# Projections of two attention layers: the order of the first segment's k held, the second x of B rounded later, A's shifts in one store, transposes of v a tile later

## The chip, the core and the metric

The kernel runs on one NeuronCore of a Trainium2 chip. The core has a matrix engine (TensorE, PE in the profile, with its weight loads as PEld), a vector engine (VectorE, DVE), an activation engine (ScalarE, ACT), a general engine (GpSimd, POOL) and a sync engine (SyncE, SP) that computes nothing and issues most of the transfers. Each engine has its own queue of instructions, which it runs in order; engines wait for each other through semaphores. SBUF is the on-chip memory of 128 partitions, PSUM the smaller one into which PE writes its sums, and DMA engines move data between SBUF and the DRAM. The metric is the device time of one execution in microseconds; lower is better.

## The reference: what is computed

Two attention layers, A and B, over 2048 positions of width 576, with 32 heads of 18; everything is float32, and the outputs are put side by side.

```python
# A: one k and one v for all heads (multi-query), no mask
q = (x @ wq).reshape(B, S, H, Dh).transpose(0, 2, 1, 3);  k = x @ wk;  v = x @ wv
p = softmax(einsum("bhqd,bkd->bhqk", q, k) * Dh ** -0.5)
a = einsum("bhqk,bkd->bhqd", p, v).transpose(0, 2, 1, 3).reshape(B, S, H * Dh) @ wo

# B: four segments of 512 positions with a memory carried from one to the next
for s in range(4):
    qs, ks, vs = q[:, :, s], k[:, :, s], v[:, :, s]
    logits = einsum("bhqd,bhkd->bhqk", qs, ks) * scale + mask
    a_dot = einsum("bhqk,bhkd->bhqd", softmax(logits), vs)
    a_mem = einsum("bhld,bhde->bhle", phi(qs), M) / (einsum("bhld,bhd->bhl", phi(qs), z)[..., None] + 1e-6)
    outs.append(g * a_mem + (1 - g) * a_dot)
    M = M + einsum("bhld,bhle->bhde", phi(ks), vs);  z = z + einsum("bhld->bhd", phi(ks))
b = stack(outs)... @ wo          # phi(t) = t + 1 if t > 0 else exp(t)
return concatenate([a, b], axis=-1)
```

## The kernel before, in words

The program has two stages. The first, until about 315 us, makes the projections q, k and v of both layers and B's memory, and puts them into DRAM; the second is attention with the output projections. The change touches the first.

**Parts.** To keep float32's accuracy at the faster matmul type, each operand is split into a rounded high part and the rest: x into `xh` and `xl` (`load_xk`, L191 to L203), the weights into `wAh`, `wAl`, `wBh`, `wBl`. A projection tile (`proj`, L232) is 14 matmuls of 512 columns into one PSUM tile `pj` (four buffers): three products for each of four slabs of 128 rows of x and two for the fifth, of 64 rows. Up to 126 rows (seven heads) come out of one tile, so a chunk of 512 positions takes five tiles.

**Layer A** (L250 on) goes through four chunks c, its tiles in the order 4, 0, 1, 2, 3. Tile 4 carries k and v besides four heads of q. ACT copies v's 18 rows to `vT` (L298), PE transposes them (L301, four small matmuls), and DVE copies them to `VA` (L302). Each tile's result is split into `qp` (ACT's cast L111, then DVE's subtraction L112; three buffers) and stored by SP (L116). Meanwhile the next chunk's x is loaded and split; in the last chunk that is B's first.

**A's shifts.** Behind the last chunk PE begins the first projection tile of B's k (`ahead`, L333). An upper bound on the scores follows: the largest k by head is spread over the rows by a matmul (L338), copied to `kAp` (L339), multiplied with a mask into `kbdA` (five steps, L342), and 20 matmuls (L347) make `pu`. From that DVE makes `fm`, `sht` and the two parts `shp` (L350, L121 to L124), which four DMAs issued by ACT store to `shA` (L353).

**Layer B** (L383 on) goes through four segments s. In each come five tiles of k (tile 4 holds the last four heads of q and three of k), eight groups of v (`values`, L457: 14 matmuls each, then ACT's copies to `vch` and `kn` and a store by ACT), and four tiles of q. For a k tile DVE takes the maximum `kmB` (L423), ACT and DVE make `qp` and SP stores it, DVE makes `kbB` (L427), then `phi` (L363): two activations `ph_e` on ACT (L366, L367) and `kf` on DVE (L369). `natural` (L393) transposes kf on PE into the one buffer `tr` (L396), and DVE copies that to `pkN` (L397). At the end of a segment, 20 matmuls (L530) give B's shifts, and `pkN` and `vch` give the memory's increment (L555, L564 on). In segment 0 the weights for q are also still being made ready: a load `wr` issued by POOL (L224), ACT's cast (L229) and POOL's subtraction (L230), one slab for each k tile.

**What sets the order.** In this stage the order of instructions on each engine is not the one written: a scheduler places each by its own estimate of when its operands are ready. `pin` (L177, `tc.keep_in_program_order`) holds those instructions that it is given in the order in which they are written; before the change these are POOL's loads, the casts and subtractions of B's weights, and a few small steps. The second stage is scheduled by hand. At its beginning all engines pass a branch on a flag (L580) that comes from the bounds.

The x of segment 1 has three load buffers `xr`. Its five slabs are written in the loop over the q tiles of segment 0 (`nx[2](t)`, L507); the scheduler puts the rounding of all five among DVE's steps of A's last tile, of A's shifts and of the first k tile.

## Time and profile before

| | us |
|---|---|
| median of 3 runs | 1448.65 |
| the runs | 1448.05 to 1451.8 |
| profiled execution | 1452.01 |
| its span | 1450.0 |
| first stage, to attention's first score matmul | 314.6 |
| PE busy in the span | 1424.0 |
| ACT busy | 1194.9 |
| DVE busy | 1023.9 |

How to read the lines of the profile shown below. A line of the stretches (two times in us with a colon) has the length, then for PE, PEld, DVE, ACT and POOL the busy time in us and the number of instructions, then the granted share of PE's clock, the busy share of the DMA engines and their GB/s. A line of the waits says which engine and line waited for whom: us in total, how often, the longest. A line of the timeline has start and duration in us, engine, line, operation, what it writes and reads, shape, how many were merged, and in brackets the idle time of that engine before it and what ended that. A matmul's duration is that of its way through the array; matmuls overlap, and the distance of their starts is what one costs. Engine names with q are that engine's issuing of transfers.

### The profile page before, as it was taken

To read this page: it belongs to the slowest core of one execution; us is meant where nothing else is said; L and a number is where in the kernel's file an instruction comes from. 1 tells how busy PE (TensorE), PEld (TensorE's weight loads), DVE (VectorE), ACT (ScalarE), POOL (GpSimd) and SP (SyncE) were. 2 spreads that over 40 slices of the span, in tenths; PEclk is the share of its full clock that TensorE was granted. 3 is DMA by queue.
4 is the path that set the end of the run, shared out by engine and by line. 5 is a ranking of instruction groups with operands and counts; after the bars stand their busy time and mean duration, and the time that the engine had idled before them with its cause. 6 is when DMAs were issued, how large, how long until landed. Compare 5 with 4: busy or idle time off the path is not lost.

```text
span 1450.0 us, 40761 instructions
## 1 busy us (share of the span) xinstructions
PE 1424.0 (98%) x17540; PEld 840.9 (58%) x17540; DVE 1023.9 (71%) x1211; ACT 1194.9 (82%) x1429; POOL 245.7 (17%) x324
## 2 busy tenths in 40 slices
PE   9989999999999999999999999999999999999998
PEld 6768878855454555555555555555555555555565
DVE  6663473556776678887777788777778877887761
ACT  4542334259999999999999999999999999999960
POOL 2421000002123312311110160131013300100001
PEclk9999999999999999999999999999999999999999
DMA  9864444457465335332312452123104121110022
GB/s 278 270 215 137 130 162 159 162 165 202 147 175 159 92 97 175 116 108 87 108 57 68 128 154 80 62 100 93 57 26 143 60 74 46 57 42 17 17 87 74
DMA packets 86079, 166.33 MB, mean 115 GB/s; under 512 B 11872, under 2 KB 19673, under 8 KB 85718
## 3 DMA queue, kind: packets, MB, share of 16 engines
q1 hardware_dynamic: 79014, 152.87, 33.8%
q0 software_dynamic: 1664, 4.78, 1.3%
q10 hardware_dynamic: 5216, 6.03, 1.3%
q8 instruction: 138, 2.26, 0.7%
q14 instruction: 47, 0.39, 0.1%
HBM read 96.15 MB, written 67.49 MB: 113 GB/s over the span
## 4 chain that ended last, share of the span: by engine, by line
PE 64%; ACT 8%; DMA 3%; issue 2%; DVE 0%; POOL 0%; SPq 0%; DVEq 0%; POOLq 0%; ACTq 0%
PE O L893 30%; PE E L845 19%; PE F L742 11%; ACT P L863 8%; PE E L854 3%; PE E L742 1%; DMA sm<-oB 1%; PE O L742 1%; DMA rB<-sm 0%; DMA rA<-sm 0%; DMA stA<-qA 0%; DMA stB<-kB 0%; DMA stB<-qB 0%; DMA out<-osb 0%; DMA rb<-rB 0%
## 5 line engine op out<-in xcount | busy, mean ns | idle before, releaser
L863 ACT ACTIVATE P<-E 128x1024 f32<-128x1024 f32 (+1 forms) x800 | 788.4, 1078 | 15.0 <-PE E L845 11.8
L860 DVE COPY W<-E 128x1024 f32<-128x1024 f32 (+1 forms) x384 | 461.0, 1201 | 188.6 <-PE E L845 121.4
L893 PE MATMUL O<-P,VA 128*32 128x256 f32 x7936 | 509.7, 380 | 0.0
L863 ACT ACTIVATE P<-W 128x1024 f32<-128x1024 f32 (+1 forms) x384 | 434.6, 1132 | 1.5 <-DVE W L860 1.5
L893 PEld LDWEIGHTS O<-P,VA 128*32 128x32 f32 x7936 | 262.6, 110 | 146.6 <-issue 9.5
L845 PE MATMUL E<-stA,kstA 56*128 56x512 f32 x1920 | 330.8, 440 | 2.0 <-ACT P L863 1.3
L845 PEld LDWEIGHTS E<-stA,kstA 56*128 56x128 f32 x1920 | 154.6, 184 | 180.8 <-ACT P L863 121.0
L868 POOL TENSOR_SCALAR_AFFINE_SELECT P<-P 128x256 f32<-128x256 f32 (+1 forms) x192 | 94.2, 493 | 447.5 <-ACT P L863 414.7
L729 POOL TENSOR_TENSOR o<-o,rb 126x512 f32<-126x512 f32 (+1 forms) x40 | 60.5, 1518 | 436.8 <-PE F L742 143.5
L742 PE MATMUL F<-woB,o 126*32 126x192 f32 (+1 forms) x1920 | 127.6, 338 | 0.0
L825 DVE SCALAR_TENSOR_TENSOR q<-q,PD 128x1024 f32<-128x1024 f32 x96 | 118.5, 1234 | 0.0
L893 PE MATMUL O<-P,vseg 128*32 128x256 f32 (+2 forms) x1536 | 83.4, 348 | 1.9 <-POOL P L868 1.8
L742 PEld LDWEIGHTS F<-woB,o 126*32 126x32 f32 (+1 forms) x1920 | 38.2, 108 | 70.8 <-issue 61.4
L742 PE MATMUL F<-woA,o 126*32 126x192 f32 (+1 forms) x1240 | 77.7, 338 | 1.3 <-DVE osb L767 1.3
L111 ACT CAST qp<-pj 126x512 fp32r<-126x512 f32 (+1 forms) x54 | 31.3, 583 | 54.6 <-DVE kmB L423 33.2
L239 PE MATMUL pj<-xh,wBh 128*126 128x512 f32 x180 | 75.0, 416 | 0.0
L902 DVE COPY oe<-O 128x512 f32<-128x512 f32 x64 | 44.2, 691 | 41.7 <-PE O L893 39.3
L239 PE MATMUL pj<-xh,wBl 128*126 128x512 f32 x180 | 72.9, 405 | 0.0
L112 DVE TENSOR_TENSOR qp<-pj,qp 126x512 fp32r<-126x512 f32 (+1 forms) x54 | 36.7, 684 | 49.7 <-ACT qp L111 49.6
L854 PE MATMUL E<-stB 56*128 56x256 f32 (+3 forms) x512 | 62.5, 350 | 2.5 <-ACT P L863 2.0
L893 PEld LDWEIGHTS O<-P,vseg 128*32 128x32 f32 x1536 | 48.6, 110 | 27.9 <-issue 3.3
L239 PE MATMUL pj<-xl,wBh 128*126 128x512 f32 x144 | 60.0, 417 | 0.0
(177 smaller groups left out, 1372.7 us busy)
## 6 DMA issues: line engine op xcount, KB each, us to landing
stB<-kB SPq DMA_DIRECT2D x96, 144.0 KB
stB<-qB SPq DMA_DIRECT2D x32, 288.0 KB
stA<-qA SPq DMA_DIRECT2D x30, 288.0 KB
oA<-oe SPq DMA_DIRECT2D x32, 256.0 KB
oB<-oe SPq DMA_DIRECT2D x32, 256.0 KB
qA<-qp SPq DMA_DIRECT2D x16, 504.0 KB
kB<-qp SPq DMA_DIRECT2D x16, 504.0 KB
qB<-qp SPq DMA_DIRECT2D x16, 504.0 KB
```

The costliest lines, as they stand in the source:

```text
L112: nc.vector.tensor_tensor(qp[:R, 1, :n], src, qp[:R, 0, :n].bitcast(F32), op=ALU.subtract)
L239: nc.tensor.matmul(dst, w[:, c0 : c0 + M], x, start=i == 0, stop=i == len(ops) - 1)
L729: steps = [lambda: v.tensor_tensor(o, o, rb, op=ALU.mult)]
L742: nc.tensor.matmul(dst[32 * j : 32 * j + 32], parts[ab, c][: RT[t], t, r0 : r0 + 32], wo[ab][: RT[t], t, c0 : c0 + n], start=start, stop=stop,
L825: steps.append(lambda a=a: v.scalar_tensor_tensor(q, q, a, p, op0=ALU.add, op1=ALU.mult))
L845: nc.tensor.matmul(e[:, j], kstA[rows, 128 * kt : 128 * kt + 128], st[rows, h, :], start=True, stop=True)
L854: nc.tensor.matmul(e[:, j, c0 : c0 + 512 - 128 * k], st[rows, 4 + h, ks], st[rows, h, 128 * k :], start=True, stop=True)
L860: nc.vector.tensor_copy(src[:, :, :n], e[:, :, :n])
L863: nc.scalar.activation(p[:, :, :n], src[:, :, :n], AF.Exp, scale=SCALE)
L868: nc.gpsimd.affine_select(diag, diag, pattern=[[0, 2], [0, m], [1, 128]], base=0, channel_multiplier=-1, compare_op=ALU.is_ge, fill=0.0)
L893: nc.tensor.matmul(o[32 * j : 32 * j + 32, q0 : q0 + n], v, p[:, j % 2, p0 : p0 + n], start=m == hf == 0, stop=last and hf == 1,)
L902: nc.vector.tensor_copy(osb, o)
```

## The change

Four edits in the first stage; the arithmetic is the same.

1. The transposes of v (L301, L302) are written under the next tile, t == 0, not directly behind tile 4. In the built order PE does them 3 to 10 matmuls later in chunks 1 to 3 and at the same place in chunk 0.
2. `shA` becomes one DRAM tensor with all four chunks' rows, and the four stores of ACT one store by SP. In the built order it stands on SP behind the last store of A's q and before the first of B's k.
3. In segment 0 of B, `hold` is `pin`: kmB, both steps of qp, kbB, and phi's three steps stand on their engines in the written order, which now has phi before `split_wpart`. In the built order DVE runs kmB, qp, kbB, kf, pkN of one tile and then those of the next; ACT runs qp, both ph_e and the cast of wr, with the copies of values between. For the later segments nothing of the sequence changes.
4. The split of segment 1's x is written behind the store of each q tile of segment 0, and its rounding is pinned (`behind=True`). In the built order all of it stands on DVE behind that tile's qp, and two of the loads on SP behind stores of q.

POOL's order is the same. PE's order differs from the first stage's chunk 1 to the values of segment 1; transposes of kn (L483) come in the first q tile of segment 0, where they stood among the values. Attention has the same instructions in the same order.

```diff
--- before.py
+++ after.py
@@ -81,7 +81,8 @@
     qB = [dram(f"qB{c}", [H, DH, 2, C], F32) for c in range(NSEG)]
     kB = [dram(f"kB{c}", [H, DH, 2, C], F32) for c in range(NSEG)]
     vB = [dram(f"vB{c}", [L, H * VW], F32) for c in range(NSEG)]
-    shA = [dram(f"shA{c}", [2, H, C], F32) for c in range(NCH)]
+    shAs = dram("shA", [2, NCH * H, C], F32)
+    shA = [shAs[:, H * c : H * c + H] for c in range(NCH)]
     shB = [dram(f"shB{c}", [2, 128, C], F32) for c in range(NSEG)]
     shX = [dram(f"shX{c}", [2, H, C], F32) for c in range(NSEG)]
     oA = [dram(f"oA{c}", [H, 32, C], F32) for c in range(NCH)]
@@ -104,12 +105,12 @@
     fm = cp.tile([128, 5], F32, name="fm")
     nc.gpsimd.memset(fm, 0.0)
 
-    def split2(pool, src, R):
+    def split2(pool, src, R, hold=lambda ins: ins):
 
         n = src.shape[-1]
         qp = pool.tile([128, 2, C], F32R, name="qp", bufs=3)
-        nc.scalar.copy(qp[:R, 0, :n], src)
-        nc.vector.tensor_tensor(qp[:R, 1, :n], src, qp[:R, 0, :n].bitcast(F32), op=ALU.subtract)
+        hold(nc.scalar.copy(qp[:R, 0, :n], src))
+        hold(nc.vector.tensor_tensor(qp[:R, 1, :n], src, qp[:R, 0, :n].bitcast(F32), op=ALU.subtract))
         return qp
 
     def store_parts(qp, r0, R, dst, h0, nh):
@@ -188,13 +189,15 @@
             tile_, c0 = XRAW[c]
             return tile_[:, k, c0 : c0 + C]
 
-        def load_xk(xh, xl, xT, c, k):
+        def load_xk(xh, xl, xT, c, k, behind=False):
             if xT is a_xT and c < 3:
                 xr = xraw(c, k)
             else:
                 xr = px.tile([128, C], F32, name="xr", bufs=3)
                 load_part(xr, xT, c * C, C, k, nc.sync)
-            (nc.scalar.copy if xT is a_xT and c == 0 else nc.vector.tensor_copy)(xh[:, k], xr)
+            rounded = (nc.scalar.copy if xT is a_xT and c == 0 else nc.vector.tensor_copy)(xh[:, k], xr)
+            if behind:
+                pin(rounded)
 
             engine = nc.gpsimd if xT is a_xT and (c, k) == (1, 3) else nc.vector
             if k < 4:
@@ -206,7 +209,7 @@
 
             xh = px.tile([128, 5, C], F32R, name="xh")
             xl = px.tile([128, 4, C], F32R, name="xl")
-            return xh, xl, lambda k: load_xk(xh, xl, xT, c, k)
+            return xh, xl, lambda k, **kw: load_xk(xh, xl, xT, c, k, **kw)
 
         def split_w(wh, wl, wr, c0, n, k, engine):
             nc.scalar.copy(wh[:, k, c0 : c0 + n], wr)
@@ -296,6 +299,8 @@
                     nc.vector.tensor_reduce(km[:M, c : c + 1], pj[:M], axis=AX.X, op=ALU.max, apply_absolute_value=True)
                     vT = p1.tile([128, C], F32, name="vT", bufs=2)
                     nc.scalar.copy(vT[96:114], pj[96:114])
+                if t == 0:
+
                     pv = ps.tile([128, 4, 128], F32, name="tr", bufs=1)
                     for i in range(4):
                         nc.tensor.transpose(pv[:, i, 0:DH], vT[96:114, 128 * i : 128 * i + 128], ident[96:114, 96:114])
@@ -349,8 +354,7 @@
                 )
         nc.vector.tensor_reduce(fm[:, 0:1], pu, axis=AX.X, op=ALU.max)
         sp = shift_parts(pt, pu, -BOUND_UP, C, 128)
-        for c in range(NCH):
-            nc.scalar.dma_start(shA[c].rearrange("j h t -> h j t"), sp[32 * c : 32 * c + 32].bitcast(F32))
+        nc.sync.dma_start(shAs.rearrange("j r t -> r j t"), sp.bitcast(F32))
         wAp.close()
 
 
@@ -360,13 +364,13 @@
         zst = p2.tile([128, 5, 32], F32, name="zst")
         zc = p2.tile([128, 5], F32, name="zc")
 
-        def phi(src, R, nm, bufs):
+        def phi(src, R, nm, bufs, hold=lambda ins: ins):
 
             e = p2.tile([128, C], F32, name="ph_e", bufs=2)
-            nc.scalar.activation(e[:R], src, AF.Relu, scale=-1.0)
-            nc.scalar.activation(e[:R], e[:R], AF.Exp, scale=-1.0)
+            hold(nc.scalar.activation(e[:R], src, AF.Relu, scale=-1.0))
+            hold(nc.scalar.activation(e[:R], e[:R], AF.Exp, scale=-1.0))
             f = p2.tile([128, C], F32, name=nm, bufs=bufs)
-            nc.vector.scalar_tensor_tensor(f[:R], src, 0.0, e[:R], op0=ALU.max, op1=ALU.add)
+            hold(nc.vector.scalar_tensor_tensor(f[:R], src, 0.0, e[:R], op0=ALU.max, op1=ALU.add))
             return f
 
         def loose_flag():
@@ -420,25 +424,27 @@
                     proj(pj[:126], wBh, wBl, xh, xl, 630 + 126 * t if t < 4 else 504, 126)
                 if t and not last:
                     natural(f, pkN[:, t - 1, :, 0:126], 0, 126)
-                nc.vector.tensor_reduce(kmB[:126, t : t + 1], pj[:126], axis=AX.X, op=ALU.max, apply_absolute_value=True)
-                qp = split2(pt, pj[:126], 126)
+
+                hold = pin if s == 0 else lambda ins: ins
+                hold(nc.vector.tensor_reduce(kmB[:126, t : t + 1], pj[:126], axis=AX.X, op=ALU.max, apply_absolute_value=True))
+                qp = split2(pt, pj[:126], 126, hold)
                 if t < 4:
                     store_parts(qp, 0, 126, kB[s], 7 * t, 7)
-                    nc.vector.tensor_scalar(kbB[:126, t], zmask[:126, t], kmB[:126, t : t + 1], None, op0=ALU.mult)
+                    hold(nc.vector.tensor_scalar(kbB[:126, t], zmask[:126, t], kmB[:126, t : t + 1], None, op0=ALU.mult))
                 else:
                     store_parts(qp, 0, 72, qB[s], 28, 4)
                     store_parts(qp, 72, 54, kB[s], 28, 3)
                     magnitude(4, pj)
+                if s and not last:
+                    nx[2](t)
+                if not last or t == 4:
+                    f = phi(pj[:126], 126, "kf" if t < 4 else "qf", 2 if t < 4 else 5, hold)
+                    if t == 4:
+                        fs[4] = f
                 if s == 0:
                     split_wpart(10 + t)
                     if t < 4:
                         load_wpart(11 + t)
-                elif not last:
-                    nx[2](t)
-                if not last or t == 4:
-                    f = phi(pj[:126], 126, "kf" if t < 4 else "qf", 2 if t < 4 else 5)
-                    if t == 4:
-                        fs[4] = f
             if s:
                 from_memory(4)
             if s == 0:
@@ -503,13 +509,13 @@
             for t in range(4):
                 pj = ps.tile([128, C], F32, name="pj", bufs=4)
                 proj(pj[:126], wBh, wBl, xh, xl, 126 * t, 126)
-                if s == 0:
-                    nx[2](t)
-                    if t == 3:
-                        nx[2](4)
                 magnitude(t, pj)
                 qp = split2(pt, pj[:126], 126)
                 store_parts(qp, 0, 126, qB[s], 7 * t, 7)
+                if s == 0:
+                    nx[2](t, behind=True)
+                    if t == 3:
+                        nx[2](4, behind=True)
                 if s:
                     fs[t] = phi(pj[:126], 126, "qf", 5)
                     from_memory(t)
```

## The prediction

> **What bounds the kernel now.** I read the page's first part and its chain first, then the stage before attention in stretches of 20 us, then TensorE's (PE's) own waits there.

> ```profile
> span 1450.0 us, 40761 instructions
> PE 1424.0 (98%) x17540; PEld 840.9 (58%) x17540; DVE 1023.9 (71%) x1211; ACT 1194.9 (82%) x1429; POOL 245.7 (17%) x324
> PE 64%; ACT 8%; DMA 3%; issue 2%; DVE 0%; POOL 0%; SPq 0%; DVEq 0%; POOLq 0%; ACTq 0%
> ...
> 60.00:80.00 20.00, 18.62 (x83) 14.40 (x81) 12.77 (x20) 8.92 (x16) 10.00 (x9) 1.00 0.83 284
> 80.00:100.00 20.00, 14.49 (x69) 10.91 (x70) 15.14 (x34) 5.50 (x11) 3.90 (x5) 0.88 0.67 199
> 100.00:120.00 20.00, 19.32 (x129) 17.59 (x129) 7.65 (x14) 9.72 (x24) 9.62 (x13) 0.95 0.50 143
> ...
> PE nd L347 <- DVE kbdA L342: 3.3, 1, 3.3
> PE tr L396 <- issue: 2.4, 1, 2.4
> PE tr L301 <- ACT vT L298: 1.2, 1, 1.2
> PE E L845 <- SPq L580: 1.1, 1, 1.1
> ```

> PE is busy 98% of the span and carries 64% of the chain, so time is won only where PE waits or runs slowly. Before attention (about 315 us) that is nearly one place: from 60 to 120 us, most of all 80 to 100, where PE is busy 14.49 of 20 us at a granted clock of 0.88. The waits are 3.3 us for kbdA, 2.4 us in front of a transpose of kf, 1.2 us for vT. The clock is a cost of its own:

> ```profile
> 61.20:64.60 3.40, 2.21 (x13) 1.52 (x12) 2.10 (x6) 1.80 (x4) 0.42 (x1) 1.00 0.98 361
> 77.90:81.30 3.40, 1.91 (x10) 1.25 (x8) 1.88 (x4) 0.00 (x0) 0.71 (x1) 1.00 0.65 248
> 81.30:84.70 3.40, 1.59 (x22) 0.87 (x23) 3.16 (x11) 0.00 (x0) 0.20 (x1) 1.00 0.82 267
> 84.80:88.20 3.40, 3.40 (x10) 2.60 (x9) 3.40 (x8) 1.10 (x2) 0.32 (x2) 0.50 0.63 196
> 94.90:98.30 3.40, 1.00 (x8) 0.92 (x8) 2.44 (x5) 2.35 (x5) 1.76 (x2) 1.00 0.30 101
> 98.40:101.80 3.40, 3.40 (x12) 2.75 (x11) 2.58 (x5) 1.64 (x4) 0.11 (x1) 0.51 0.72 230
> ```

> Two stretches of 3.4 us run at half clock, each right behind one in which PE idled 1.8 us (81.3) or 2.4 us (94.9); idling 1.2 and 1.5 us (61.2, 77.9) had no such sequel. A half-clock stretch loses 1.7 us of work. Waits and clock together: 3.3 + 2.4 + 1.2 + 2 x 1.7 = 10.3 us, and that is about all there is to win.

> **Where the two large waits come from.** VectorE (DVE) and ScalarE (ACT) run in order; the built order of the changed kernel shows what stands before what.

> ```profile
> 79.42 0.43 DVE L197 CAST xh<-xr 128x512 fp32r<-128x512 f32 x1 [3.53 <-DMA xr<-b_xT]
> ...
> 82.63 0.15 DVE L339 COPY kAp<-mm 126x1 f32<-126x1 f32 x1
> 82.81 0.82 DVE L342 TENSOR_SCALAR kbdA<-hmask,kAp 126x32 bf16<-126x32 f32 x5
> ...
> 78.50 0.28 PE L338 MATMUL mm<-kmx,sel 114*126 114x1 f32 x2
> 78.64 0.48 PE L239 MATMUL pj<-xh,wBh 128*126 128x512 f32 x1
> 83.11 1.26 PE L347 MATMUL nd<-AQ,kbdA 126*32 126x512 bf16 x20 [3.30 <-DVE kbdA L342]
> ...
> 95.84 0.68 DVE L112 TENSOR_TENSOR qp<-pj,qp 126x512 fp32r<-126x512 f32 x1
> 96.44 0.68 DVE L369 SCALAR_TENSOR_TENSOR kf<-pj,ph_e 126x512 f32<-126x512 f32 x1
> ...
> 75.95 0.58 ACT L111 CAST qp<-pj 126x512 fp32r<-126x512 f32 x1
> 87.83 3.54 ACTq L353 DMA_DIRECT2D shA<-shp  x4
> 91.50 0.60 ACT L366 ACTIVATE ph_e<-pj 126x512 f32<-126x512 f32 x1 [3.65 <-DMA shA<-shp]
> ...
> 139.67 0.41 SPq L535 DMA_DIRECT2D shB<-shp  x1
> ```

> kAp could go at 78.8 (78.50 + 0.28), but DVE stood 3.53 us at a rounding of segment 1's x whose load had not landed, and then did four more x steps: kAp came at 82.63. kf of the first tile of k came at 96.44, behind maxima of later tiles that waited for PE, and its ph_e (91.50) behind four stores that held ACT's queue 3.54 us.

> **The change, part by part.** Times are on the scale of the profiled run; a DVE step on a whole tile follows the last after 0.60 us (95.84 to 96.44), a projection matmul of PE takes 0.233 (56 in 13.04), a values matmul 0.133 to 0.138 (46 in 6.23), and one tile of k, held in order, costs what segment 1 shows:

> ```profile
> 122.01:135.05 13.04, 13.04 (x56) 10.23 (x56) 1.00 0.39 128
> 115.64:121.87 6.23, 6.23 (x46) 6.23 (x47) 1.00 0.38 38
> ...
> 154.31 0.69 DVE L423 TENSOR_REDUCE kmB<-pj 126x1 f32<-126x512 f32 x1 [0.71 <-PE pj L239]
> 155.65 0.68 DVE L112 TENSOR_TENSOR qp<-pj,qp 126x512 fp32r<-126x512 f32 x1
> 157.66 0.69 DVE L369 SCALAR_TENSOR_TENSOR kf<-pj,ph_e 126x512 f32<-126x512 f32 x1 [0.58 <-ACT ph_e L367]
> 158.54 0.59 PE L396 MATMUL tr<-ident,kf 126*128 126x126 f32 x4
> 159.17 0.68 DVE L397 COPY pkN<-tr 128x504 f32<-128x504 f32 x1 [0.22 <-PE tr L396]
> ```

> kmB to the end of kf is 158.35 - 154.31 = 4.04 us (it alternates with ACT's qp and two ph_e steps, which all read one PSUM tile in turn), transposes to pkN 0.63, pkN to the next kmB 0.60: 5.3 us a tile.

> *Transposes of v a tile later.* PE waits 1.2 us for vT where they stand now; with the rest of a tile, 10 matmuls or 2.3 us, put between, vT is there first. -1.2 us, and all that follows moves with it. If that cover were gone the 1.2 us would be back. Nothing waits for VA before attention.

> *x of segment 1 rounded late.* kAp at 78.8, kbdA from 79.0, the matmuls of L347 0.3 later (82.81 to 83.11) at 79.3; PE has three projection matmuls from 78.64, so it arrives at 79.3 too: the 3.3 us and the half clock behind them go (-5.0). Late next would be DVE's qp of A's last tile: ACT casts it by 76.5 (75.95 + 0.58), so DVE is free at 77.3. The price comes in the q stage, below.

> *One store for A's shifts.* ACT is free of 3.54 us of issuing. SP has one issue (0.41 us for the like store of L535) between a store of q and one of k; it waits for shp at 83.1, the k store behind it is not ready before 85.0. The same bytes travel. No time of its own: it only lets ph_e follow.

> *k held in order.* fm, sht, shp run from 80.6 to 83.1, kmB of tile 0 at 83.0, and each tile's pkN must now come before the next kmB. Walking the queues, with PE leaving L347 at 80.5:
> - tile 0: kf done 87.05; PE reaches its transposes after 30 matmuls at 87.5. No wait.
> - tile 1: kmB 88.8, kf 92.8; PE at 93.0. No wait.
> - tile 2: kmB 94.2, kf 98.6, since ACT's copy of the first values stands before its ph_e. PE's second values group needs that copy's buffer: wait 0.8, and 0.35 before the transposes at 98.6.
> - tile 3: kmB 99.8, kf 104.0; PE at 103.9. Tile 4: qf 110.4; PE at 110.3. Waits of 0.1 each.
> - the q projections begin at 111.2; before, at 122.01. Gain 10.8 with kbdA's part in it.

> So the 2.4 us wait and its half clock go, and 1.35 us of small waits come. The unknown here is the load of wr, which is pinned behind POOL's step and in front of ACT's next cast:

> ```profile
> DMA to landing us min/median/max: 3.0/5.7/8.2
> ...
> 89.16 0.57 POOL L224 DMA_DIRECT2D wr<-b_w  x1
> 97.60 0.56 POOL L224 DMA_DIRECT2D wr<-b_w  x1
> ...
> 95.70 0.61 ACT L229 CAST wBh<-wr 128x504 fp32r<-128x504 f32 x1 [2.60 <-DMA wr<-b_w]
> 100.99 0.61 ACT L229 CAST wBh<-wr 128x504 fp32r<-128x504 f32 x1 [0.50 <-DMA wr<-b_w]
> ```

> The first of these took 6.5 us (89.16 to 95.70), the next 3.4 (97.60 to 100.99). At 3.4 throughout, the walk stands. With 6.5 for the first alone, ACT reaches tile 2's qp 0.5 us late, all later loads come 2.7 us late, and the q projections begin at 113.05: 1.9 us worse. I take 0.7 of these, nearer to the short landing, since the loads of segment 1's x that shared the DMA engines then have moved away.

> *The q stage.* The transposes of kn and their small matmul move into it: +0.65. x steps now follow each qp on DVE; the fourth and fifth tile's land on DVE at 129.2 to 132.4 while PE, at the first tile of segment 1, asks for them at 131.2 and 132.6 (q done at 126.8 in the later case). No wait, by 0.2 us. Behind it DVE is fuller: PE comes to the memory products of L555 and to the first transposes before DVE has read the product before or made kf, in four waits of 1.2 us together; between the same two points the old order loses 0.45: +0.75. Segments 1 to 3 and attention keep their orders, so what is won stays won.

> Sum: -1.2 (v) - 10.8 + 0.65 (k, values, kn) + 0.75 (segment 1) + 0.7 (wr) = -9.9 us. The profiled execution took 1452.0 (span 1450.0 and 2.0 around it), 3.4 above the median of the three runs; from the median 1448.65 I get 1438.7. Ends: no new wait at all, -12.7, is 1436; the first load late and the clock halved twice more, -8.7 + 3.4, is 1443.3.

> **The rivals.**
> - *Two stretches stay at half clock,* from the new small waits, or because the old waits were not what halved it. For it: four waits within 93 to 110 us and four more behind the q stage. Against: 1.2 and 1.5 us of idling in one stretch had no sequel, and mine add up to 1.2 in a stretch; 1.8 and 2.4 us were each followed at once. Two such stretches cost 3.4: 1442.1. [...]
> - *The wr loads stay slow.* If all four land after 6.5 us, each holds ACT in front of the next copy of values, PE waits about 3 us at the last two, and the q projections begin near 119.5: 8.3 worse than the walk, gain 2.5, 1446. For it: a median of 5.7 us; against it: 3.4 in this very stage.
> - *Slower: the held chain becomes the bound.* DVE may start no kmB before PE has done the transposes of the tile before. At 5.3 us a tile it keeps pace; break-even is where the q projections begin at 122.6 (122.01 + 1.2 - 0.65), which is (122.6 - 83.0 - 6.0) / 4 = 8.4 us a tile, with 6.0 from the last kmB to them. At 9 us PE idles about 3 us a tile, which also halves its clock four times: + 2.4 + 6.8, 1458. For it: PE's transposes stand at fixed places and ACT's queue has casts of weights and copies of values between a tile's steps. Against: segment 1's 5.3 us was measured with such company.
> - *Nothing changes:* the start of attention follows something other than PE. There PE waited 1.1 us for the branch on the flag, which follows PE's last products; no load stood in its way.

> **How the numbers follow.** Forecast 0.62; clock 0.12; wr slow in part or whole 0.12, of which 0.07 is still faster and 0.05 within 0.3%; held chain 0.09; unchanged 0.05. About 0.3% (4.3 us) is what runs of this kernel can tell from no change. Faster 0.62 + 0.12 + 0.07 = 0.81, same 0.10, slower 0.09. The range runs from 1436 to 1445, past the clock case and into the slow loads; the likeliest case alone is 1436 to 1441.

> **What would show it.** Right: no wait of PE for kbdA, granted clock 1.00 from 80 to 120, the q stage's first projection near 110 us (111.2 - 1.2), waits of PE under 1.2 us at L467 and L396, attention's first E near 304. Wrong: DVE waiting at pkN for PE while PE waits at the next transposes; ACT waiting for wr over 2 us twice; a stretch at 0.50 between 85 and 125.

## The result and the profile after

| | median us | lowest to highest | kernel before beside it, same chip | ratio, 95% interval |
|---|---|---|---|---|
| changed kernel | 1442.35 | 1436.14 to 1445.79 | 1448.98 | 0.9949, 0.9934 to 0.9964 |
| changed kernel, another time (`after_2` below) | 1437.96 | 1437.28 to 1439.99 | 1450.59 | 0.9911, 0.9886 to 0.9936 |

The change is faster, by 7 to 13 us: the prediction was 1438.7, 9.9 under the median before. The two rows are the same program. The ratio is an estimate from all runs and not the quotient of the two medians, so it differs a little from that. Before attention the profiled executions of the two rows differ in one place, and most of what follows is about that place.

The changed kernel's first profile has a span of 1441.6 us (its time 1444.52). The waits of PE in it, from 60 to 130 us (in total, how often, the longest):

```profile
PE nd L352 <- DVE kbdA L347: 1.9, 1, 1.9
PE pj L473 <- ACT kn L477: 0.6, 1, 0.6
```

and its stretches of 20 us:

```profile
80.00:100.00 20.00, 19.17 (x102) 14.96 (x102) 10.27 (x22) 6.30 (x12) 4.08 (x6) 0.91 0.48 169
100.00:120.00 20.00, 19.86 (x135) 18.18 (x134) 8.36 (x16) 11.15 (x26) 9.62 (x13) 1.00 0.58 164
```

The stretch from 80 to 100 us has PE busy 19.17 us instead of 14.49. The waits for vT and for kf are gone, but 1.9 us of the wait for kbdA stayed, and the clock is still 0.91. The lines of the changed kernel stand one to six lower than those of before (L342 is now L347, L347 is L352, L396 is L400), and in the kernels of the experiments they shift again; the tiles' names stay. The stretches of the second profile:

```profile
80.00:100.00 20.00, 19.28 (x105) 16.38 (x104) 10.94 (x20) 8.21 (x17) 5.33 (x6) 1.00 0.48 165
100.00:120.00 20.00, 20.00 (x126) 17.84 (x125) 8.62 (x17) 10.34 (x24) 7.85 (x11) 1.00 0.58 151
```

and one row of its timeline:

```profile
304.23 1.06 PE L851 MATMUL E<-st,kstA 56*128 56x512 f32 x6 [0.98 <-SPq L586]
```

Here the clock is 1.00 throughout, there is no wait for kbdA, and E, attention's first score matmul, comes at 304.23, where it came at 314.63 before and at 307.87 in the first profile. The prediction had said "near 304".

**Where the two executions part.** The timeline of the first profile, a row for each engine concerned (start, duration, engine, line):

```profile
74.78 0.59 ACT L112 CAST qp<-pj 126x512 fp32r<-126x512 f32 x1 [3.21 <-DMA kA<-qp]
...
77.54 0.59 ACT L112 CAST qp<-pj 126x512 fp32r<-126x512 f32 x1 [1.10 <-DMA qA<-qp]
...
78.16 0.69 DVE L113 TENSOR_TENSOR qp<-pj,qp 126x512 fp32r<-126x512 f32 x1 [2.07 <-ACT qp L112]
78.76 0.15 DVE L344 COPY kAp<-mm 126x1 f32<-126x1 f32 x1
78.95 1.85 DVE L347 TENSOR_SCALAR kbdA<-hmask,kAp 126x32 bf16<-126x32 f32 x5
...
78.78 1.39 POOL L233 TENSOR_TENSOR wBl<-wr,wBh 128x576 fp32r<-128x576 f32 x1 [0.84 <-ACT wBh L232]
...
80.26 1.96 PE L352 MATMUL nd<-AQ,kbdA 126*32 126x512 bf16 x20 [1.90 <-DVE kbdA L347]
```

and the same rows of the second:

```profile
77.48 0.16 DVE L344 COPY kAp<-mm 126x1 f32<-126x1 f32 x1 [1.47 <-PE mm L343]
77.68 0.82 DVE L347 TENSOR_SCALAR kbdA<-hmask,kAp 126x32 bf16<-126x32 f32 x5
...
76.21 1.44 POOL L233 TENSOR_TENSOR wBl<-wr,wBh 128x576 fp32r<-128x576 f32 x1
...
78.18 1.26 PE L352 MATMUL nd<-AQ,kbdA 126*32 126x512 bf16 x20
```

Two things went wrong in the first. kAp came 1.3 us later, behind the last qp of A, because ACT's casts waited for stores out of qp's three buffers to land. Then the five kbdA steps took 1.85 us instead of 0.82: the first of them started 0.17 us into POOL's subtraction of a slab of B's weights and ended 0.04 us behind it. In the second execution POOL was done at 77.65, 0.03 us before kbdA began.

The stores were late for the same reason, 12 us earlier. The timeline there, DVE's x steps, POOL's subtractions and SP's store of k, in the first profile and the second:

```profile
64.89 1.42 POOL L233 TENSOR_TENSOR wBl<-wr,wBh 128x576 fp32r<-128x576 f32 x1 [3.24 <-ACT wBh L232]
64.98 1.88 DVE L204 TENSOR_TENSOR xl<-xr,xh 128x512 fp32r<-128x512 f32 x1
66.78 2.15 DVE L198 CAST xh<-xr 128x512 fp32r<-128x512 f32 x1
...
67.19 1.45 POOL L233 TENSOR_TENSOR wBl<-wr,wBh 128x576 fp32r<-128x576 f32 x1
...
71.07 0.79 SPq L323 DMA_DIRECT2D kA<-qp  x1
```

```profile
64.25 0.69 DVE L204 TENSOR_TENSOR xl<-xr,xh 128x512 fp32r<-128x512 f32 x1
...
64.77 1.46 POOL L233 TENSOR_TENSOR wBl<-wr,wBh 128x576 fp32r<-128x576 f32 x1 [3.24 <-ACT wBh L232]
65.11 1.40 DVE L198 CAST xh<-xr 128x512 fp32r<-128x512 f32 x1 [0.17 <-DMA xr<-b_xT]
...
68.66 0.79 SPq L323 DMA_DIRECT2D kA<-qp  x1
```

In the first, a load of x had landed 0.7 us later, so xl met POOL's step and took 1.88 us instead of 0.69; the cast behind it met the next one and took 2.15 (0.43 where it meets none; in the second profile it met the earlier step of POOL and took 1.40). The release of xr, SP's next loads and the store of k behind them on SP's queue all moved, by 1.9 to 2.4 us.

The traces of the experiments below, which have much the same steps up to here, bear this out. With each shifted so that PE's first matmul of A's second chunk falls where the second profile has it, the cast xh behind that load starts at 63.10 to 63.82 us in `after_2`, `pool_away`, `pool_away_2`, `two_ahead` and `no_pool`, and the store of k is issued at 67.8 to 68.7; it starts at 64.35 to 64.81 in the first profile, `no_store`, `no_k`, `both` and `late_kbdA`, and the store is issued at 70.9 to 71.2. PE waits for kbdA in every trace of the second group (in `late_kbdA` by its edit as well) and in none of the first. Of the others, `free_act` falls between (64.24; a later load delays its store to 72.7), and `no_v` and `no_x` have another order of steps here.

### The profile page after: what moved, and what is told of

Read it like the earlier page. It is cut to its first block, busy times and chain, and to the rows that moved or that the text cites. A ratio compares the mean times of both kernels' runs of the same rounds, so it can differ in the third digit from the quotient of the medians.

```text
span 1441.6 us, 40756 instructions
## 1 busy us (share of the span) xinstructions
PE 1420.8 (99%) x17540; PEld 843.5 (59%) x17540; DVE 1026.7 (71%) x1211; ACT 1195.2 (83%) x1429; POOL 243.9 (17%) x324
## 4 chain that ended last, share of the span: by engine, by line
PE 65%; ACT 8%; issue 3%; DMA 1%; DVE 1%; POOL 0%; SPq 0%; DVEq 0%; POOLq 0%; ACTq 0%
PE O L899 30%; PE E L851 19%; PE F L748 12%; ACT P L869 8%; PE E L860 3%; PE E L748 1%; DMA oB<-oe 1%; PE O L748 1%; DVE W L866 0%; DMA o<-oB 0%; POOL o L735 0%; DVE PD L824 0%; DVE oe L908 0%; DVE PD L827 0%; DVE q L828 0%
## 5 line engine op out<-in xcount | busy, mean ns | idle before, releaser
L831 DVE SCALAR_TENSOR_TENSOR q<-q,PD 128x1024 f32<-128x1024 f32 x96 | 119.5, 1245 | 0.0
L112 ACT CAST qp<-pj 126x512 fp32r<-126x512 f32 (+1 forms) x54 | 31.3, 583 | 59.9 <-DVE kmB L429 39.4
```

What stands on the lines that cost most here:

```text
L831: steps.append(lambda a=a: v.scalar_tensor_tensor(q, q, a, p, op0=ALU.add, op1=ALU.mult))
```

## The experiments

Each row is a kernel with its median, the kernel before timed beside it, and from its one profiled execution PE's wait for kbdA and the time from PE's first matmul of A's second chunk to the first q projection of B. That distance is used because in three of the traces (`no_store`, `free_act`, `two_ahead`) PE reached that chunk 1.4 to 1.8 us later than in `after_2`. In `no_k` and `late_kbdA`, as before the change, the distance has 0.9 us of kn's transposes in it, which the others have behind the first q projection.

| | median | before | ratio, 95% interval | wait for kbdA | to first q |
|---|---|---|---|---|---|
| before | | | | 3.3 | 99.05 |
| changed, first profile | 1442.35 | 1448.98 | 0.9949, 0.9934 to 0.9964 | 1.9 | 91.39 |
| `after_2` | 1437.96 | 1450.59 | 0.9911, 0.9886 to 0.9936 | none | 87.79 |
| `no_v` | 1442.58 | 1449.36 | 0.9943, 0.9922 to 0.9964 | none | 89.44 |
| `no_store` | 1441.79 | 1449.36 | 0.9940, 0.9917 to 0.9963 | 1.5 | 91.08 |
| `no_x` | 1447.03 | 1449.36 | 0.9978, 0.9963 to 0.9994 | 5.0 | 95.06 |
| `no_k` | 1445.34 | 1449.36 | 0.9969, 0.9954 to 0.9983 | 1.0 | 95.98 |
| `pool_away` | 1437.53 | 1451.83 | 0.9912, 0.9891 to 0.9933 | none | 87.76 |
| `free_act` | 1437.74 | 1451.83 | 0.9911, 0.9891 to 0.9932 | 2.0 | 91.21 |
| `two_ahead` | 1441.34 | 1451.83 | 0.9936, 0.9915 to 0.9958 | none | 89.79 |
| `pool_away_2` | 1438.34 | 1450.59 | 0.9912, 0.9887 to 0.9936 | none | 87.71 |
| `both` | 1437.56 | 1450.59 | 0.9909, 0.9884 to 0.9934 | 0.5 | 88.35 |
| `late_kbdA` | 1447.21 | 1450.59 | 0.9980, 0.9962 to 0.9998 | 3.6 | 97.34 |
| `no_pool` | 1438.49 | 1449.30 | 0.9923, 0.9899 to 0.9946 | none | 87.83 |

### One part of the change undone at a time

**The transposes of v back behind tile 4.**

```diff
-                if t == 0:
-
-                    pv = ps.tile([128, 4, 128], F32, name="tr", bufs=1)
+                    pv = ps.tile([128, 4, 128], F32, name="tr", bufs=1)
```

> After with the transposes of v back behind tile 4. Theory (each part adds its own): PE waits 1.2 us for vT again and everything behind it comes 1.2 us later, A's matmul on kmx at 78.5 instead of 77.3, the first q projection at 115.6 instead of 114.4; time 1.2 us over the changed kernel. Rival (covered): in the changed kernel kAp comes at 78.8 from DVE's and ACT's queues and not from PE, so that the 1.2 us are spent inside the wait for kbdA, which shrinks from 1.9 to 0.7; time the same as the changed kernel, first q projection at 114.4.

Of its waits of PE:

```profile
PE tr L305 <- ACT vT L301: 1.6, 1, 1.6
```

The wait is back, at 1.6 us. From the second chunk to the matmul on kmx PE takes 55.95 us instead of 54.23, and to the first q 1.65 more than in `after_2`: the theory's row. Yet against the first profile this kernel's q is nearer by 1.95, because here kbdA met no step of POOL. By time it is not told apart from the changed kernel.

**A's shifts in four stores by ACT.** Here shA is four tensors again, and:

```diff
-        nc.sync.dma_start(shAs.rearrange("j r t -> r j t"), sp.bitcast(F32))
+        for c in range(NCH):
+            nc.scalar.dma_start(shA[c].rearrange("j h t -> h j t"), sp[32 * c : 32 * c + 32].bitcast(F32))
```

> After with the four stores of A's shifts on ACT again. Theory (the stores stand in front of the first k tile's cast on ACT): issuing takes ACT 3.5 us from 84.7, the cast moves from 85.4 to 88.3, kf of tile 0 from 88.1 to 91.0; PE waits 1.5 us at the first transposes and the first q projection comes 2 to 4 us later (116.5 to 118.5), the upper end with a half-clock stretch behind the wait. Rival (cover): the chain has slack enough, no wait over 0.5 us, q projection at 114.4 to 115.

Its timeline for ACT, and the wait of PE that follows:

```profile
85.00 1.81 ACTq L357 DMA_DIRECT2D shA<-shp  x4
86.86 0.59 ACT L111 CAST qp<-pj 126x512 fp32r<-126x512 f32 x1 [7.36 <-issue]
```

```profile
PE tr L400 <- DVE kf L373: 1.7, 2, 1.6
```

The theory's mechanism with half its size: the issuing took 1.81 us here and not 3.54, the cast followed at 86.86, and PE waited 1.6 us, though at the second tile's transposes (96.92) and not at the first. From the first projection behind kbdA to the first q it is 33.1 us against 31.4 in `after_2`. Its time cannot be told from the changed kernel's.

**The x of segment 1 where the scheduler puts it.** In the q loop `nx[2](t)` stands behind `proj` again, and without `behind=True`.

> After with the x of segment 1 rounded where the scheduler puts it, among A's last tiles. Theory: DVE stands at a rounding whose load has not landed, kAp at 82 to 83 instead of 78.8, PE's wait for kbdA 3 us or more instead of 1.9, and all behind it 2 to 3 us later: first q projection near 117; nothing is won back in the q stage, where the late rounding cost PE nothing. Rival (the wait is set by ACT's casts and POOL, not by x): kbdA at 80.3 as in the changed kernel, first q projection near 114.4.

Its timeline for DVE, and the wait of PE that follows:

```profile
79.70 0.43 DVE L198 CAST xh<-xr 128x512 fp32r<-128x512 f32 x1 [4.87 <-DMA xr<-b_xT]
```

```profile
PE nd L352 <- DVE kbdA L347: 5.0, 1, 5.0
```

DVE stands 4.87 us at the load and kAp comes at 82.91, as before the change. This part is worth 7.3 us of distance against `after_2` and 3.7 against the first profile, and 0.3 to 0.7% of time, by which of the two rows of the changed kernel one compares with.

**The first segment's k not held.** `hold` is the identity, and phi stands behind `split_wpart` again.

```diff
-                hold = pin if s == 0 else lambda ins: ins
+                hold = lambda ins: ins
```

> After with the first segment's k not held. Theory: kf late on DVE behind maxima of later tiles, a wait of PE of 2 us or more at a transpose between 90 and 105, a half-clock stretch behind it, first q projection 4 us later (118.5), time +4. Rival (the store and x were enough to free ACT and DVE): no wait over 1 us there, first q projection within 1 us of 114.4, time the same as the changed kernel; part of the rival: with no held chain the small waits of 0.7 and 0.3 us go too, 113.4.

Its waits of PE at the transposes:

```profile
PE tr L400 <- DVE kf L373: 4.5, 2, 3.0
PE tr L400 <- DVE qf L373: 1.1, 1, 1.1
```

From the first projection behind kbdA to the first q it takes 38.5 us instead of 31.4; 0.9 of these 7.1 are kn's transposes, which stand ahead of the first q again (13.04 us from there to B's first bounds matmul instead of 13.90). The rival falls, but the half-clock stretch that the theory expected didn't come either. So the hold and the late x carry the gain, and the two other parts 1.7 us each in the traces, under what the times resolve. In the times `no_x` and `no_k` are both slower than `after_2`; from the first row of the changed kernel the interval of `no_x` all but parts, and `no_k` isn't told apart. The four parts aren't additive: undone singly they cost some 17 us of distance together, where the whole change gave 10.4 (both without kn's 0.9). In `no_x`, for one, PE waits 5.0 us for kbdA and not the 3.3 of before, since the 1.3 us won at vT are lost there again.

### What made kbdA late

**One subtraction moved from POOL to DVE**, the slab whose step ran beside kbdA:

```diff
+            rest = (wBl[:, k, c0 : c0 + n], wrs[i], hi.bitcast(F32))
+            if i != 9:
+                pin(nc.gpsimd.tensor_tensor(*rest, op=ALU.subtract))
...
+            pin(nc.vector.tensor_scalar(kbd[:126, t], hmask[:126, t], kAp[:126], None, op0=ALU.mult))
+        pin(nc.vector.tensor_tensor(*rest, op=ALU.subtract))
```

> After with one of POOL's subtractions of B's weights (the slab whose step overlapped kbdA) done by DVE behind kbdA instead. Theory (DVE's step from SBUF to SBUF is slow while POOL subtracts): the first kbdA step takes 0.24 us instead of 1.26, kbdA is there 1.0 us earlier, PE's wait before its 20 matmuls falls to 0.9 us or less and no half-clock stretch follows; first projection behind them at 81.2 instead of 82.2, first q projection at 111.7 to 112.5 instead of 114.4. Rival (the first kbdA step is slow for another reason, such as its first read of hmask or its scalar): it still takes 1.2 to 1.5 us, and nothing moves.

Its kbdA steps, and below them those of `no_k`, which does the same work up to there but with POOL's step beside it:

```profile
77.54 0.16 DVE L347 COPY kAp<-mm 126x1 f32<-126x1 f32 x1 [1.00 <-PE mm L346]
77.73 0.82 DVE L350 TENSOR_SCALAR kbdA<-hmask,kAp 126x32 bf16<-126x32 f32 x5
```

```profile
77.47 0.16 DVE L344 COPY kAp<-mm 126x1 f32<-126x1 f32 x1
77.67 2.09 DVE L347 TENSOR_SCALAR kbdA<-hmask,kAp 126x32 bf16<-126x32 f32 x5
...
77.71 1.42 POOL L233 TENSOR_TENSOR wBl<-wr,wBh 128x576 fp32r<-128x576 f32 x1
```

With kAp at the same time the five steps take 0.82 us without POOL and 2.09 with it. That is the theory, and q comes at 110.76. In `no_k` the first kbdA step, 1.51 of the 2.09 us, ends 0.05 us behind POOL's.

**A buffer of its own for the fourth chunk's first qp.**

```diff
-                qp = split2(pt, pj[:R2], R2)
+                qp = split2(pt, pj[:R2], R2, qp=st0[:, 0:2] if (c, t) == (3, 4) else None)
```

> After with a buffer of its own for the fourth chunk's first qp (in st0, which is free until attention), so that ACT's later casts of A's q need not wait for that store to land. Theory (the three buffers of qp hold ACT, and through it DVE and kAp): ACT has no wait over 1 us for a store between 70 and 78, the last qp of A stands on DVE by 77.2 and kAp comes at 77.7, as soon as PE has its product, instead of 78.8; kbdA then 1 us earlier, if POOL's step does not move along with it. Rival (ACT waits for loads or PE as well): kAp stays at 78.5 or later.

Two rows of its timeline, DVE's and ACT's:

```profile
71.04 1.94 DVE L204 TENSOR_TENSOR xl<-xr,xh 128x512 fp32r<-128x512 f32 x1
...
80.55 0.59 ACT L112 CAST qp<-pj 126x512 fp32r<-126x512 f32 x1 [2.76 <-DMA qA<-qp]
```

The profile misses the theory: three x steps met POOL again (the one shown and casts of 1.62 and 1.06 us), ACT's wait went from the store of k to the next store of q, and PE itself stood 1.1 us at 73.6 for a PSUM tile that DVE had not yet read. That execution was the slowest of the six (1441.42 us); the runs, at 0.9911, are as fast as any. The buffers pass lateness on; they do not begin it.

**The second k tile's projection ahead of the matmuls that use kbdA.**

```diff
+        ahead1 = ps.tile([128, C], F32, name="pj", bufs=4)
+        pin(proj(ahead1[:126], wBh, wBl, xh, xl, 756, 126))
         kbd = p1.tile([128, 5, 32], BF, name="kbdA")
```

> After with the whole of the second k tile's projection (14 matmuls instead of 3) in front of the matmuls that use kbdA. Theory (the wait that stayed cost 1.9 us of PE and a half-clock stretch): kbdA is there when PE comes, at 80.6; no wait, no half clock; the held chain of k still starts at 84.5, so that its slack decides: first q projection at 111.5 to 113, time 1.5 to 3 us under the changed kernel. Rival (the held chain is by now the bound): PE's idling moves to the transposes of tiles 0 to 2, 1.5 us and more, first q projection at 114 or later, time the same as the changed kernel.

Its largest wait of PE between 60 and 130 us:

```profile
PE tr L403 <- DVE kf L376: 1.6, 1, 1.6
```

No wait for kbdA and no half clock, but 1.6 us at the second tile's transposes: the rival. The matmuls come at 82.51, 2.2 us after kbdA's last step; fm, sht, shp and with them the held chain of k stand behind them on DVE, which cost 2.0 us of distance against `after_2`. Its median lies 3.8 us over that of `pool_away`, timed beside it.

**The changed kernel once more, and the subtraction on DVE once more, with and without the buffer.**

> The changed kernel once more, beside the others on one chip. Theory (kbdA falls on POOL's subtraction or beside it, by where ACT's casts happen to end): its first kbdA step is 1.2 to 1.5 us in an execution where it overlaps POOL's step, and PE waits 1.0 to 2.0 us; the runs of this kernel spread wider than those of the kernel with that subtraction moved, and its median lies 2 to 5 us over it. Rival (the difference between the two was the chip's): the two medians lie within 1 us.

> The kernel with that one subtraction on DVE once more. Theory: first kbdA step 0.24 us, no wait for kbdA, no half-clock stretch between 70 and 130, first q projection near 110.8, median 2 to 5 us under the changed kernel on the same chip. Rival: as for the changed kernel once more.

> The subtraction on DVE and the own buffer for the fourth chunk's first qp together. Theory (once POOL is out of the way kbdA comes right behind PE's product, and ACT's waits for stores no longer reach it): the same as the subtraction alone within 1 us. Rival (the buffer gives something of its own, as its median of 1437.7 alone let hope): 2 us or more under the subtraction alone.

The three medians, 1437.96, 1438.34 and 1437.56, lie within 0.8 us. The difference between 1442.35 and 1437.53 that had spoken for the moved subtraction was one of occasion, as the rival said. In `after_2` no step of POOL met kbdA, and the changed kernel is as fast as the others; three casts of x met POOL there too (1.40, 0.96 and 1.05 us), without reaching kAp. In the profile of `both` ACT still waited 2.3 us for a store of q, and PE 0.5 us for kbdA: without POOL's step lateness still reaches it, but costs less. No version was shown to beat the changed kernel.

**All five subtractions of A's last chunk on DVE**, `engine = nc.vector if 5 <= i < 10 else nc.gpsimd`.

> After with all five subtractions of B's weights in A's last chunk on DVE instead of POOL. Theory (in the first profile of the changed kernel two x steps of DVE, at 65.0 and 66.8 us, took 1.88 and 2.15 us beside POOL's subtractions instead of 0.69 and 0.43, and passed that on through the buffers of xr and qp, SP's stores and ACT's casts to kbdA): no DVE step on SBUF over 1.0 us between 62 and 80, the store of the fourth chunk's k issued by SP at 68 to 70, kAp within 0.6 us of PE's product, no half-clock stretch between 70 and 130, first q projection at 110.5 to 112 on any chip, median 11 to 13 us under the kernel before. Rival (DVE is too full for 5 more steps of 0.75 us): the last qp of A stands on DVE after 78.5, kAp at 79 or later, PE waits for kbdA 1 us or more.

Two rows of its timeline, DVE's and SP's:

```profile
64.27 0.69 DVE L204 TENSOR_TENSOR xl<-xr,xh 128x512 fp32r<-128x512 f32 x1
...
67.75 0.79 SPq L324 DMA_DIRECT2D kA<-qp  x1
```

As the theory has it: between 62 and 80 us no x step is slowed, the store of k is issued at 67.75 and kAp comes at 77.73, with 0.75 us of DVE for each slab. The median, 10.8 us under the kernel before, is no better than that of `after_2`. One profile shows no collision here; that it holds wherever the changed kernel collides is argued, not shown, since no trace has both side by side.

### What a wait of PE costs

**kbdA delayed on purpose**, in the kernel with the moved subtraction, and with the second tile's projection pinned behind:

```diff
+        for _ in range(4):
+            pin(nc.vector.tensor_scalar(idle[:126], ahead[:126], 1.0, None, op0=ALU.mult))
         kbd = p1.tile([128, 5, 32], BF, name="kbdA")
```

> The subtraction on DVE, and four extra steps of DVE (each 0.6 to 0.7 us, on a tile that nobody reads) between kAp and kbdA, with the second k tile's projection behind the matmuls that use kbdA: PE stands idle some 3.2 us for kbdA and has nothing else to do. Theory (PE idle for more than about 1.7 us within one 3.4 us window of the clock's grid is followed by one window at half clock): a stretch at 0.50 right behind the wait, its start a whole number of 3.413 us from any other such stretch of the same trace; first q projection near 115.6 (110.8 + 2.4 of wait + 0.7 of matmuls moved + 1.7). Rival (a whole idle window is needed): no such stretch, 113.9, unless the wait happens to fill one window of the grid.

Stretches of one window each (PE's busy time is the first number behind the length, its clock the first share):

```profile
76.79:80.20 3.41, 0.74 (x5) 0.55 (x3) 2.72 (x5) 1.16 (x3) 1.55 (x2) 1.00 0.89 297
80.20:83.61 3.41, 2.47 (x21) 0.93 (x22) 2.19 (x9) 0.00 (x0) 0.01 (x1) 0.50 0.75 270
83.61:87.03 3.42, 3.42 (x9) 2.63 (x10) 2.91 (x5) 0.36 (x1) 0.33 (x1) 0.50 0.10 38
100.69:104.10 3.41, 1.51 (x12) 1.27 (x11) 1.15 (x4) 1.99 (x5) 1.13 (x1) 1.00 0.59 205
104.10:107.52 3.42, 3.42 (x16) 3.42 (x15) 2.05 (x4) 1.06 (x3) 0.64 (x2) 0.50 0.28 83
```

Besides kbdA, PE waited once more from 84 us on:

```profile
PE pj L480 <- ACT kn L484: 1.9, 1, 1.9
```

The half clock followed the wait, so the rival falls; but there are three such windows, not one, and the first q came at 120.37 and not near 115.6. The third stands behind the wait for kn, and not behind that for kbdA. The delay of kbdA's matmuls was 2.9 us (81.14 against 78.23). The time paid was 8.9 us (1447.21 against 1438.34): about the delay, 1.7 for each of the three windows (half of 3.41; projection matmuls start 0.43 us apart from 84.41 to 86.54 and 0.23 from 87.24 on), and the 1.1 us by which PE's later waits are longer than in `after_2`. The edit also moved other matmuls, kn's transposes among them, so that not all of this need be the price of the one wait.

Two more windows, each with the one behind it: one of `no_k`, and one of `after_2` at the start of attention.

```profile
91.53:94.94 3.41, 1.54 (x9) 1.38 (x10) 2.84 (x5) 2.16 (x4) 1.28 (x2) 1.00 0.38 78
94.94:98.35 3.41, 3.22 (x19) 2.52 (x17) 1.80 (x4) 1.90 (x4) 1.79 (x2) 1.00 0.39 157
```

```profile
305.06:308.47 3.41, 2.13 (x12) 0.83 (x10) 3.19 (x4) 3.41 (x4) 0.14 (x1) 1.00 0.24 64
308.47:311.88 3.41, 3.41 (x28) 1.43 (x28) 3.26 (x3) 3.41 (x5) 0.00 (x0) 0.50 0.74 184
```

Half-clock windows of one trace start a whole number of 3.413 us apart (before: 84.79 and 316.89, 68 windows; first profile after: 80.69, 312.79 and 439.09, 68 and 37; `late_kbdA`: 80.20 and 104.10, 7). Read by what PE did within one window of that spacing, busy 0.74 and 1.51 us were followed by half clock, 1.54 was not. The last two are close, and the profile models the ends of PE's matmuls; that a bound lies near 1.5 us is an estimate from these three windows, and the last section has windows that it does not sort. The wait of 3.0 us in `no_k`, from 90.43 to 93.40, lies across the edge at 91.53, and no half clock followed it.

## Why the prediction was right, and where it was not

- **The path.** It was PE's in the stage before attention, as said. Of the first profile's 8.4 us of span, 6.8 are won before attention's first E; of the second's 13.7, 10.4 are. The rest are half-clock windows in attention: three before, two and one after, 1.7 us each. The prediction had nothing of these, so 1.6 and 3.3 us of the gain came by luck.
- **Transposes of v, -1.2.** Right: 55.53 us before and 54.23 after, from the second chunk to the kmx matmul, -1.3; 1.7 by `no_v`.
- **x rounded late, "the 3.3 us and the half clock behind them go (-5.0)".** This is the step that the first profile shows wrong. The matmuls on kbdA started at 80.26 instead of 78.1 (79.3, less the 1.2 of v), PE still waited 1.9 us, and 80.69 to 84.10 ran at half clock. Of 5.0 us, 1.4 came: 3.3 - 1.9 of wait, none of the clock. What failed is the sentence on what is late next, "ACT casts it by 76.5, DVE is free at 77.3": it left out that a cast of ACT needs a buffer of qp, hence a landed store, and that a subtraction of POOL may run beside kbdA (1.85 us instead of 0.82). In the second profile of the same program ACT's wait for the store of k was 1.6 us instead of 3.2 and did not reach kAp, POOL's step was over, the matmuls started at 78.18 and the -5.0 held. So the term depends on the execution, and as far as the traces tell, 0.7 us in one load's landing decides between the two. Why the load lands late was not looked into. How often each comes up isn't known from two profiles; the medians fit the second value on one occasion and lie nearer to the first on the other.
- **One store by SP, "no time of its own".** Right for the store. That it frees ACT was worth 1.7 us (`no_store`), which the prediction had inside the hold.
- **k held in order, 5.3 us a tile.** The best part. With PE out of kbdA's matmuls at 80.5 the walk put the transposes at 87.5, 93.0, 98.6, 103.9 and 110.3. In `after_2` PE leaves them at 79.44, 1.06 us sooner:

```profile
86.38 0.59 PE L400 MATMUL tr<-ident,kf 126*128 126x126 f32 x4
...
97.71 0.65 PE L400 MATMUL tr<-ident,kf 126*128 126x126 f32 x4 [0.16 <-DVE kf L373]
...
109.90 0.60 PE L400 MATMUL tr<-ident,qf 126*128 126x126 f32 x4
```

  With the second at 91.94 and the fourth at 103.24, each is within 0.7 us of the walk shifted by 1.06, and the first q, at 110.73, too. The waits there are 0.6 (values behind kn's copy) and 0.2, where 1.35 was put. The drift lies mostly in PE's own matmuls: from the third transposes to the fifth it had no wait and took 12.2 us, where the walk had 11.7 (98.6 to 110.3). The 5.3 us a tile came out as 5.5 to 5.8 (kmB starts at 81.89, 87.61, 93.18, 99.00 and 104.52); the sum had left out the piece from kf's end to the transposes (158.35 to 158.54 in its own rows).
- **Loads of wr, +0.7.** All five landed after 2.5 to 2.9 us in the first profile and ACT waited for none, so nothing came of them, and the rival of slow loads falls. By luck the walk's drift used the term up.
- **kn's transposes and small matmul, +0.65.** First q to B's first bounds matmul was 13.04 and is 13.90: +0.86.
- **Segment 1, +0.75.** Did not come: from those bounds to segment 1's first values it is 22.78 before and 22.77 after.
- **The rivals.** One of the "two stretches" that stay at half clock did stay, in the first profile alone, though not for the reason given: an old wait that survived, no new ones. A window did not have to be idle throughout for it: the one of `late_kbdA` with 1.51 us of busy PE was followed by half clock. The held chain did not become the bound, but it runs level with PE: in `after_2` kf is done 0.06 to 0.4 us ahead of four of the five transposes, and PE waits 0.2 us at the other. In `two_ahead`, where the matmuls on kbdA and with them the chain start 2.5 us later on the same scale, PE waited 1.6 us for it.

The terms close, with the drift set against the term for wr: -9.9, less the 0.75 of segment 1, plus 0.2 for kn, is -10.45, and E shows -10.4 in the second profile; in the first, 3.6 us of kbdA's 5.0 are missing (91.39 against 87.79), and E shows -6.8. Of the time, by the ratios, the change gave -7.4 and -12.9 us of 1448.65, on both sides of the -9.9. Of the signs that the prediction named for being right, the second profile has every one; the first has only the short waits at the values and the transposes of kf.

## What to carry to other kernels

When a wait is taken away, follow the next one back through buffers too: here an engine that casts into a rotating buffer waited up to 3.2 us for the store out of it to land. Keep steps like POOL's subtractions out of the way of DVE's on SBUF: a cast of x that met one took 2.15 us instead of 0.43 and ended 0.29 us behind it, and a chain of buffers handed that on for 12 us. Price a wait of TensorE by what it leaves of a 3.41 us window as well as by its length, since 1.51 us of busy PE in one was followed by a window at half clock, 1.7 us lost, and the wait of 3.0 us in `no_k` by none. And take a second profile before one execution's wait is explained by the program.
